# First weight of a fused attention and feed-forward kernel read in 8 pieces of 1024 columns, and two PE transposes a stage later

## The chip, the cores and the metric

The kernel runs on one core of one Trainium2 chip. A core has TensorE (PE, matrix products, with the loading of its stationary operand shown apart as PEld), VectorE (DVE), ScalarE (ACT), GpSimd (POOL) and SyncE (SP, which here only issues transfers). Each engine executes its own list of instructions in order and waits on semaphores where it needs another engine or a transfer. The metric is the device time of one execution in microseconds, the median of three runs.

## The reference

Block-sparse attention of 4 batches, 8 heads, 768 positions, 64 numbers per head, followed by layer norm and a feed-forward layer with a residual. In short:

```python
scores = q @ k.T / sqrt(64)                 # masked: blocks of 32 keys
mask = |block_i - block_j| <= 1, first and last block, 3 sampled blocks per query block
attn = exp(scores - max) / (sum + 1e-9)
x = attn @ v                                # 4 x 768 x 512
xn = (x - mean) / sqrt(var + 1e-6) * g_ln
out = x + relu(xn @ w_ch1) @ w_ch2          # w_ch1 512 x 2048, w_ch2 2048 x 512
```

The two weights come as 64-bit floats, the other tensors in 32 bits.

## The kernel before

**Steps and units.** A batch has 6 tiles of 128 queries. A unit is a pair of tiles, (1,2), (3,4) or (0,5); a step is one tile with one half of the heads, so unit 0 holds steps 0 to 3, unit 1 steps 4 to 7, and step 8 begins unit 2. A step multiplies scores (`scores` or, for the first and last block, `dense_scores`, into `ps`), takes maxima (L391), exponentials (L400), turns the weights (in the first eight steps on PE, L405; later by a DMA transpose), splits them into a high and a low half in 16 bits (`pt`, L410 and L417, or `pw`, L412 and L419) and multiplies with gathered V (`pa`, L454). Gathered V (`vg`) comes from DRAM by transfers of SP and by indirect transfers of POOL (L314); in steps 1 and 2 POOL first copies the maxima of the step to come (`fence`, L312), so that its gathers start no earlier. `rc` (L438) starts the normalisation of `pa` into x.

**Order.** The program's order is written out by hand in the loop over steps at the end of the kernel function: between the parts of a step stand positions pre, a, b, c, d, e, f, at which `hook` runs what is entered there. A weight piece is entered at one position; its load is issued by `pump` up to ten positions ahead (`LEAD`), as soon as its place is free.

**Weights.** A piece is one load of SP (L158) and one conversion: three integer operations on DVE (L172, L174, L176) make a 32-bit float `wf` of the 64-bit one, ACT writes its 16-bit high half (L186, into `w1h` or `w2h`), DVE its rest (L181, into `w1l` or `w2l`). `high()` and `low()` issue the last two when the loop calls them. Before, w1 has 16 pieces and w2 16, each 128 x 512 numbers or 512 KB. Pieces 0 to 2 are converted in step 0, pieces 3 to 31 at positions a, b, c, d of steps 1 to 7 and at a of step 8. Pieces are landed in `raw` (three buffers, shared with q, K and V of later batches) or in quarters of `w2h` and `w2l` that are still unused (`HOME`); `wf` has a pool of three.

**Feed-forward.** `layer_norm` is a generator of three stages: statistics; then the normalised input xn (L511) and, for units 0 and 1 (`XPE`), its four transposes on PE (L517, into `px`); then the copy of `px` into `xT` in two halves (L520, L521). Later units transpose by DMA. In step i the loop calls the stages of tile i-1: statistics behind b, the second at c, the third behind d. `ffn` makes up-projection (`pu`, L546, eight tiles of 24 matmuls), its relu in two halves (`hh` on ACT L558, `hl` on DVE L559) and down-projection (`pd`, L575), one matmul at a time, and the loop draws a planned number of them between its parts (`run`, `part`): for unit 0, 78 per step from step 4 on. `px`, `pu` and `pd` share three places in PSUM (`ps_f`), taken by turns; a tile must wait until the one three before it is read out. The V of batch 0 is staged in `st_hh` and `st_hl` (`hst`), whose memory becomes `hh` and `hl` when the feed-forward starts; stores to DRAM read it at the start of the program (L253).

Of the kernel before, what the change touches and what calls it, by code (L numbers as in the profile page):

```python
# [26 lines left out]
def sparse_attention_moe(  # L27
# [114 lines left out]

    def weight(i):
        if i < NW1:
            fq, c = divmod(i, CT)
            src = w1[c * P : (c + 1) * P, fq * 512 : (fq + 1) * 512]
            dh, dl = (w[:, c, fq * 512 : (fq + 1) * 512] for w in (w1h, w1l))
            return src, dh, dl, gs[:, c : c + 1]
        f = i - NW1
        return w2[f * P : (f + 1) * P, :], w2h[:, f, :], w2l[:, f, :], SW2  # L150

    HOME = {3: 3, 4: 4, 5: 5, 6: 6, 7: 7, 8: 0, 9: 1, 10: 2, 11: 3, 12: 4, 13: 5, 14: 6, 15: 7, 16: 1, 17: 2,
            18: 3, 19: 5, 20: 6, 21: 7, 22: 2, 23: 3, 24: 7, 25: 3, 26: 7, 27: 3}
# [14 lines left out]
    def convert_w(i):  # L168
        _, dh, dl, scale = weight(i)
        raw = wraw.pop(i).rearrange("p (e t) -> p e t", t=2)  # L170
        wf = wfp.tile([P, 512], I32, tag="wf", name=f"wf{i}")
        nc.vector.tensor_scalar(out=wf, in0=raw[:, :, 1], scalar1=3, scalar2=0x3FFFFFFF,  # L172
                                op0=ALU.logical_shift_left, op1=ALU.bitwise_and)
        nc.vector.scalar_tensor_tensor(out=wf, in0=raw[:, :, 1], scalar=-0x40000000, in1=wf,  # L174
                                       op0=ALU.bitwise_and, op1=ALU.bitwise_or)
        nc.vector.scalar_tensor_tensor(out=wf, in0=raw[:, :, 0], scalar=29, in1=wf,  # L176
                                       op0=ALU.logical_shift_right, op1=ALU.bitwise_or)
        f = wf.bitcast(F32)

        def to_low():  # L180
            nc.vector.scalar_tensor_tensor(out=dl, in0=f, scalar=scale, in1=dh, op0=ALU.mult,  # L181
                                           op1=ALU.subtract)
            wdone.append(i)

        def to_high():
            nc.scalar.activation(dh, f, AF.Copy, scale=scale)  # L186
# [18 lines left out]
    hst = [hp.tile([P, 4096], F16, tag=tag, name=f"st_{tag}") for tag in ("hh", "hl")]  # L205
# [291 lines left out]
    def layer_norm(u, k):  # L497
        b, t = u.b, u.ts[k]
        x = xs[b, t]
        nm = f"{b}_{t}"  # L500
        if k == 0:
            u.xT = lnp.tile([P, CT, 2, 2 * P], F16, tag="xT", name=f"xT{u.i}", bufs=2)
        bs = sm.tile([P, 6], F32, tag="bs", name=f"bs{nm}")
        mv = sm.tile([P, 4], F32, tag="mv", name=f"mv{nm}")
        nc.vector.bn_stats(bs, x)
        nc.vector.bn_aggr(mv[:, 0:2], bs)
        nc.scalar.activation(mv[:, 2:3], mv[:, 1:2], AF.Ln, bias=eps, scale=1.0)
        nc.scalar.activation(mv[:, 2:3], mv[:, 2:3], AF.Exp, scale=-0.5)
        yield
        xn = wfp.tile([P, DM], F32, tag="wf", name=f"xn{nm}")  # L510
        nc.vector.tensor_scalar(out=xn, in0=x, scalar1=mv[:, 0:1], scalar2=mv[:, 2:3],  # L511
                                op0=ALU.subtract, op1=ALU.mult)
        at = slice(k * P, (k + 1) * P)
        if u.i < XPE:
            pt = ps_f.tile([P, DM], F32, tag="pf", name=f"px{nm}")
            for c in range(CT):
                nc.tensor.transpose(pt[:, c * P : (c + 1) * P], xn[:, c * P : (c + 1) * P], ident)  # L517
# [5 lines left out]
        yield  # L523
# [9 lines left out]
    def ffn(u):  # L533
# [3 lines left out]
        for f in range(0, FT, 2):  # L537
            ph = ps_f.tile([P, 512], F32, tag="pf", name=f"pu{u.i}_{f}")
            for j in range(2):
                fs = slice((f + j) * P, (f + j + 1) * P)  # L540
                n = 0
                for c in range(CT):
                    for w, k in ((w1h, 0), (w1l, 0), (w1h, 1)):
                        while u.i == 0 and f // 4 * CT + c not in wready:
                            yield True
                        nc.tensor.matmul(ph[:, j * 2 * P : (j + 1) * 2 * P], w[:, c, fs],  # L546
                                         xT[:, c, k, :], start=n == 0 and j == 0,
                                         stop=n == 3 * CT - 1, skip_group_check=True)
                        n += 1
                        if n < 3 * CT or j == 0:  # L550
                            yield
            if late:
                late.pop()()

            def hidden(f=f, ph=ph):
                dh = hh[:, f : f + 2, :].rearrange("p f n -> p (f n)")
                dl = hl[:, f : f + 2, :].rearrange("p f n -> p (f n)")
                nc.scalar.activation(dh, ph, AF.Relu)  # L558
                nc.vector.scalar_tensor_tensor(out=dl, in0=ph, scalar=0.0, in1=dh,  # L559
                                               op0=ALU.max, op1=ALU.subtract)  # L560
# [69 lines left out]

    POS = ("pre", "a", "b", "c", "d", "e", "f")
    LEAD = 10
    PAT = {}

    def place(n):
        return n + (1 if n < NPE else LAG)
# [55 lines left out]
    def item(i, p, home, load, convert):  # L692
        n = index(i, p)

        def free():
            busy[home] -= 1

        def run_convert():
            gen = convert()
# [7 lines left out]

    def pump(now):
        blocked = set()
        for it in sorted(loads):  # L710
            n, _, home, load = it
            if n > now + LEAD:
                break
            if home in blocked or busy.get(home, 0) >= (3 if home == "raw" else 1):
                blocked.add(home)
                continue
            busy[home] = busy.get(home, 0) + 1
            load()
            loads.remove(it)

# [84 lines left out]
    i = 0  # L805
    while i < NS + LAG + FFLAG + 1 or ffq:
# [21 lines left out]
        if i < NPE:  # L828
# [5 lines left out]
            if i == 0:  # L834
# [181 lines left out]
```

## Time and profile before

| what | value |
|---|---|
| median of 3 runs | 801.84 us (798.68 to 802.06) |
| the profiled execution's own time | 802.09 us |
| its span | 800.1 us, 26387 instructions |
| PE busy | 684.5 us (86%), 11088 matmuls |
| DVE busy | 493.4 us (62%), 900 instructions |
| ACT busy | 465.4 us (58%), 1201 instructions |
| POOL busy | 173.8 us (22%) |
| HBM read and written | 89.18 MB and 12.95 MB |

Busy time is the sum over an engine's instructions; a share of the span is an average over stages with different limits. In the slices each digit is the busy share of a fortieth of the span in tenths. In the timeline a row has start, duration, engine, line, operation, what is written and read, and in brackets the idle time ahead of it with what ended it. The chain of waits is followed back from the last instruction, at each step to what released it or to the instruction ahead on its engine. "issue" means that the engine waited for nothing that the profile shows.

### The profile page before, as it was taken

To read this page: it belongs to the slowest core of one execution; us is meant where nothing else is said; L and a number is where in the kernel's file an instruction comes from. 1 tells how busy PE (TensorE), PEld (TensorE's weight loads), DVE (VectorE), ACT (ScalarE), POOL (GpSimd) and SP (SyncE) were. 2 spreads that over 40 slices of the span, in tenths; PEclk is the share of its full clock that TensorE was granted. 3 is DMA by queue.
4 is the path that set the end of the run, shared out by engine and by line. 5 is a ranking of instruction groups with operands and counts; after the bars stand their busy time and mean duration, and the time that the engine had idled before them with its cause. 6 is when DMAs were issued, how large, how long until landed. Compare 5 with 4: busy or idle time off the path is not lost.

```text
span 800.1 us, 26387 instructions
## 1 busy us (share of the span) xinstructions
PE 684.5 (86%) x11088; PEld 448.8 (56%) x11088; DVE 493.4 (62%) x900; ACT 465.4 (58%) x1201; POOL 173.8 (22%) x189
## 2 busy tenths in 40 slices
PE   0343376879887899999999899999999999999998
PEld 0232255536643584674865765847748658477573
DVE  5797979846756676556575765665666655444220
ACT  4764555345777786555767875566778655432110
POOL 0134410110205332203134231121343311110000
PEclk9999979799988999999999999999999999999999
DMA  8996646347969999997479999874699994541100
GB/s 287 267 298 204 181 126 201 114 113 150 226 146 207 221 231 205 212 188 185 112 169 216 234 201 245 174 191 115 129 212 212 199 193 103 141 101 29 53 1 27
DMA packets 196022, 136.36 MB, mean 170 GB/s; under 512 B 139584, under 2 KB 174912, under 8 KB 195904
## 3 DMA queue, kind: packets, MB, share of 16 engines
q1 hardware_dynamic: 186496, 110.69, 59.2%
q0 software_dynamic: 8448, 23.44, 12.3%
q8 instruction: 87, 1.43, 0.8%
q10 hardware_dynamic: 960, 0.54, 0.2%
q14 instruction: 31, 0.25, 0.1%
HBM read 89.18 MB, written 12.95 MB: 128 GB/s over the span
## 4 chain that ended last, share of the span: by engine, by line
PE 63%; DVE 17%; ACT 7%; DMA 6%; issue 5%; ACTq 1%; SPq 1%; DVEq 0%
PE pd L575 27%; PE pu L546 23%; PE pa L454 4%; PE ps L337 3%; DVE st L391 2%; DMA vdr<-vs 2%; PE pd L481 2%; DVE wf L174 2%; PE ps L343 2%; ACT ka L291 2%; PE ps L378 1%; DVE ka L235 1%; DVE wf L176 1%; DVE pw L419 1%; ACT ps L400 1%
## 5 line engine op out<-in xcount | busy, mean ns | idle before, releaser
L314 POOL DMA_INDIRECT vg<-vdr,vidx x176 | 172.4, 979 | 512.6 <-PE pa L454 334.4
L546 PE MATMUL pu<-xT,w1h 128*128 128x256 f16 x1536 | 264.5, 276 | 10.7 <-DMA xT<-xh 3.1
L546 PE MATMUL pu<-xT,w1l 128*128 128x256 f16 x768 | 211.8, 276 | 0.0
L546 PEld LDWEIGHTS <-w1h 128*128 128x128 f16 x1536 | 150.8, 99 | 29.0 <-issue 5.0
L575 PE MATMUL pd<-w2h,hh 128*128 128x512 f16 x384 | 148.6, 387 | 0.3 <-DVE hl L559 0.3
L575 PE MATMUL pd<-w2l,hh 128*128 128x512 f16 x384 | 148.1, 386 | 0.0
L575 PE MATMUL pd<-w2h,hl 128*128 128x512 f16 x384 | 147.8, 385 | 0.0
L400 ACT ACTIVATE ps<-ps,st 128x256 f32<-128x256 f32 (+1 forms) x176 | 85.6, 486 | 102.7 <-DVE st L392 78.4
L291 ACT COPY ka<-ka 128x128 f16 x576 | 123.2, 295 | 8.3 <-issue 6.8
L575 PEld LDWEIGHTS <-hh 128*128 128x128 f16 x768 | 71.7, 99 | 82.4 <-issue 8.7
L559 DVE SCALAR_TENSOR_TENSOR hl<-pu,hh 128x512 f16<-128x512 f32 x96 | 65.5, 687 | 71.2 <-ACT hh L558 62.3
L558 ACT ACTIVATE hh<-pu 128x512 f16<-128x512 f32 x96 | 56.1, 592 | 68.3 <-PE pu L546 65.0
L419 DVE TENSOR_TENSOR pw<-ps,pw 128x1024 f16<-128x1024 f32 (+1 forms) x56 | 64.3, 1148 | 46.2 <-ACT pw L412 37.4
L391 DVE TENSOR_REDUCE st<-ps 128x4 f32<-128x1024 f32 (+1 forms) x64 | 73.7, 1152 | 29.8 <-PE ps L378 17.3
L546 PEld LDWEIGHTS <-w1l 128*128 128x128 f16 x768 | 75.9, 99 | 16.6 <-issue 5.8
L454 PE MATMUL pa<-vg,pt 128*32 128x65 f16 (+1 forms) x4224 | 53.1, 200 | 13.8 <-issue 13.8
L575 PEld LDWEIGHTS <-hl 128*128 128x128 f16 x384 | 38.1, 99 | 47.0 <-issue 3.0
L454 PEld LDWEIGHTS <-pt 128*32 128x32 f16 x4224 | 44.7, 98 | 32.1 <-issue 30.2
L412 ACT CAST pw<-ps 128x1024 f16<-128x1024 f32 (+1 forms) x56 | 52.8, 944 | 0.5
L274 DVE TENSOR_TENSOR ql<-qr,qx 64x512 f16<-64x512 f32 x44 | 30.2, 686 | 26.3 <-ACT qx L273 19.3
L405 PE MATMUL ps<-ident,pw 128*128 128x128 f32 x64 | 13.1, 371 | 28.1 <-ACT pw L400 21.6
L581 DVE SCALAR_TENSOR_TENSOR ot<-pd,x 128x512 f32<-128x512 f32 x24 | 16.4, 686 | 32.1 <-PE pd L575 32.0
(83 smaller groups left out, 626.6 us busy)
## 6 DMA issues: line engine op xcount, KB each, us to landing
vg<-vdr SPq DMA_DIRECT2D x32, 390.0 KB
w2l<-w SPq DMA_DIRECT2D x13, 512.0 KB
va<-vdr SPq DMA_DIRECT2D x8, 780.0 KB
w2h<-w SPq DMA_DIRECT2D x12, 512.0 KB
out<-ot SPq DMA_DIRECT2D x24, 256.0 KB
qr<-qs SPq DMA_DIRECT2D x22, 256.0 KB
vg<-vdr SPq DMA_DIRECT2D x16, 292.5 KB
vdr<-vs SPq DMA_DIRECT2D x36, 130.0 KB
```

What stands on the lines that cost most here:

```text
L274: nc.vector.tensor_sub(ql[rows], raw[rows], qx[rows, j])
L291: nc.scalar.copy(kg[:, :, n], kxs[b, hg][:, :, bass.ds(val, 1)].rearrange("p j o q k -> p j (o q) k"))
L314: nc.gpsimd.indirect_dma_start(vg[:, qb - 4 * s.t, 1, :], None, src[:, :], bass.IndirectOffsetOnAxis(ap=vidx[:, qb : qb + 1], axis=0))
L391: nc.vector.tensor_reduce(out=s.st[:, 0 : s.m], in_=s.parts, axis=AX.X, op=ALU.max)
L400: nc.scalar.activation(to[:, k], s.parts[:, k], AF.Exp, bias=s.st[:, k : k + 1], scale=0.125)
L412: nc.scalar.copy(s.pw[:, 0, 0 : s.n], s.whole)
L419: nc.vector.tensor_sub(s.pw[:, 1, 0 : s.n], s.whole, s.pw[:, 0, 0 : s.n])
L454: nc.tensor.matmul(pa[gr * BLK : (gr + 1) * BLK, hl * 66 : hl * 66 + n], s.pt[:, ch + c, half, gr * BLK : (gr + 1) * BLK], s.vg[:, gr, c, ...
L546: nc.tensor.matmul(ph[:, j * 2 * P : (j + 1) * 2 * P], w[:, c, fs], xT[:, c, k, :], start=n == 0 and j == 0, stop=n == 3 * CT - 1, skip_gr ...
L558: nc.scalar.activation(dh, ph, AF.Relu)
L559: nc.vector.scalar_tensor_tensor(out=dl, in0=ph, scalar=0.0, in1=dh, op0=ALU.max, op1=ALU.subtract)
L575: nc.tensor.matmul(po, x[:, f, cols], w[:, f, :], start=f == 0 and n == 0, stop=f == FT - 1 and n == 2)
```

## The change

w1 now comes in 8 pieces of 1024 columns (1 MB each), so that w1 and w2 together have 24 pieces. Pieces 0 and 1 are converted in step 0, pieces 2 to 7 at positions a and c of steps 1 to 3, and the 16 pieces of w2, as wide as before, at a, b, c, d of steps 4 to 7; nothing is entered in step 8 any more. Pieces 0 and 1 are landed in rows of `w1l` and `w1h` that are written later, the others of w1 in two neighbouring quarters of `w2h` or `w2l`, so a place can be a tuple. The 32-bit float of a w1 piece stands in `st_hh` and `st_hl` by turns. And in `layer_norm` the second stage ends behind xn: the four transposes stand at the start of the third.

```diff
-    NW1, NW = CT * FT // 4, CT * FT // 4 + FT
+    hst = [hp.tile([P, 4096], F16, tag=tag, name=f"st_{tag}") for tag in ("hh", "hl")]
+    WC = 1024
+    NW1 = CT * DF // WC
+    NW = NW1 + FT
+    w1g, w1m = (x.rearrange("p c n -> p (c n)") for x in (w1h, w1l))
     def stage(i):
-        if i in HOME:
-            t, n = divmod(HOME[i], 4)
-            return (w2f, w2g)[t][:, n * 2048 : (n + 1) * 2048].bitcast(I32)
-        return rawp.tile([P, 1024], I32, tag="raw", name=f"wr{i}")
+        n = 2 * (WC if i < NW1 else DM)
+        if i < 2:
+            return (w1m, w1g)[i][:, DF : DF + 2 * n].bitcast(I32)
+        if HOME[i][0] == "raw":
+            return rawp.tile([P, n], I32, tag="raw", name=f"wr{i}")
+        t, k = divmod(HOME[i][0], 4)
+        return (w2f, w2g)[t][:, k * 2048 : k * 2048 + 2 * n].bitcast(I32)
...
+    HOME = {2: (4, 5), 3: (0, 1), 4: (2, 3), 5: (6, 7), 6: (4, 5), 7: (0, 1), 8: (2,), 9: (3,), 10: (6,), 11: (7,),
+            14: (2,), 15: (3,), 17: (7,), 19: (3,)}
+    HOME = {i: HOME.get(i, ("raw",)) for i in range(2, NW)}
...
     def convert_w(i):
-        wf = wfp.tile([P, 512], I32, tag="wf", name=f"wf{i}")
+        if i < NW1:
+            wf = hst[i % 2][:, 0 : 2 * WC].bitcast(I32)
+        else:
+            wf = wfp.tile([P, DM], I32, tag="wf", name=f"wf{i}")
...
         at = slice(k * P, (k + 1) * P)
+        yield
         if u.i < XPE:
             pt = ps_f.tile([P, DM], F32, tag="pf", name=f"px{nm}")
             for c in range(CT):
                 nc.tensor.transpose(pt[:, c * P : (c + 1) * P], xn[:, c * P : (c + 1) * P], ident)
-            yield
             src = pt.rearrange("p (c n) -> p c n", n=P)
...
-                        while u.i == 0 and f // 4 * CT + c not in wready:
+                        while u.i == 0 and f * P // WC * CT + c not in wready:
...
-    for i in range(3):
+    for i in range(2):
         load_w(i)
-    busy["raw"] = 3
+    busy.update({h: 1 for h in (0, 1, 2, 3, 6, 7)})
...
-    WPOS = [None] * 3 + [(i, p) for i in range(1, 9) for p in PAT.get(i, "abcd")]
+    WPOS = [None] * 2 + [(i, p) for i in range(1, 4) for p in "ac"] + [(i, p) for i in range(4, 8) for p in "abcd"]
```

`pump`, `item` and the step-0 code are changed to match (a tuple of places is free when each of its places is; piece 2 is no longer converted in step 0).

Three places in the engines' orders show what moves. On DVE, step 1 up to the second maximum (`st`), before; `wf` is the 32-bit float, `pt` the low half of step 1's weights:

```order
L172 TENSOR_SCALAR wf_630<-w2l 128x512
L174 SCALAR_TENSOR_TENSOR wf_630<-w2l,wf_630 128x512
L176 SCALAR_TENSOR_TENSOR wf_630<-w2l,wf_630 128x512
L181 SCALAR_TENSOR_TENSOR w1l<-wf_413,gs,w1h 128x512
L181 SCALAR_TENSOR_TENSOR w1l<-wf_485,gs,w1h 128x512
L417 TENSOR_TENSOR pt_636<-ps_371,pt_636 128x8x128
```

and with the change at the same place, where `st_hh` takes the part of `wf`:

```order
L183 TENSOR_SCALAR st_hh<-w2l 128x1024
L185 SCALAR_TENSOR_TENSOR st_hh<-w2l,st_hh 128x1024
L187 SCALAR_TENSOR_TENSOR st_hh<-w2l,st_hh 128x1024
L192 SCALAR_TENSOR_TENSOR w1l<-st_hh,gs,w1h 128x1024
L427 TENSOR_TENSOR pt_615<-ps_363,pt_615 128x8x128
```

The rest `w1l` of a piece now follows the integer operations of the same piece; before, those of two earlier pieces did. On PE, in step 6 around the transposes of tile 3 (`px_3`), before:

```order
L546 LDWEIGHTS w1l
L546 MATMUL pu_12_1985<-xT_869,w1l 128x256
L517 MATMUL px_3_2012<-ident,xn_3_2010 128x128 x4
L546 LDWEIGHTS w1h
L546 MATMUL pu_12_1985<-xT_869,w1h 128x256
```

and with the change:

```order
L555 LDWEIGHTS w1h
L555 MATMUL pu_14_1967<-xT_831,w1h 128x256
L528 MATMUL px_3_1987<-ident,xn_3_1953 128x128 x4
L555 LDWEIGHTS w1h
L555 MATMUL pu_14_1967<-xT_831,w1h 128x256
```

The transposes stand 19 matmuls of the up-projection later, in the middle of its last tile `pu_14` instead of in `pu_12`. Those of tile 4 in step 8 stand six matmuls of the down-projection later; else PE's order is the same. On DVE in step 8, from its maxima (`st`) to the normalisation (`rc`) of step 7's `pa`, before:

```order
L391 TENSOR_REDUCE st_2277<-ps_2260 128x1
L392 TENSOR_SCALAR st_2277<-st_2277 128x1
L181 SCALAR_TENSOR_TENSOR w2l<-wf_2241,w2h 128x512
L172 TENSOR_SCALAR wf_2318<-wr_2204 128x512
L174 SCALAR_TENSOR_TENSOR wf_2318<-wr_2204,wf_2318 128x512
L176 SCALAR_TENSOR_TENSOR wf_2318<-wr_2204,wf_2318 128x512
L181 SCALAR_TENSOR_TENSOR w2l<-wf_2318,w2h 128x512
L438 TENSOR_SCALAR rc_4_1_0_2435<-pa_2338 128x4
```

and with the change:

```order
L401 TENSOR_REDUCE st_2220<-ps_2203 128x1
L402 TENSOR_SCALAR st_2220<-st_2220 128x1
L192 SCALAR_TENSOR_TENSOR w2l<-wf_2184,w2h 128x512
L448 TENSOR_SCALAR rc_4_1_0_2372<-pa_2275 128x4
L449 RECIPROCAL rc_4_1_0_2372<-rc_4_1_0_2372 128x4
```

The conversion of one w2 piece is gone from there; it stands in step 7 now.

More of the change, by code (lines that the diff above doesn't have):

```diff
@@ L145, in weight @@
             fq, c = divmod(i, CT)
-            src = w1[c * P : (c + 1) * P, fq * 512 : (fq + 1) * 512]
-            dh, dl = (w[:, c, fq * 512 : (fq + 1) * 512] for w in (w1h, w1l))
-            return src, dh, dl, gs[:, c : c + 1]
+            at = slice(fq * WC, (fq + 1) * WC)
+            return w1[c * P : (c + 1) * P, at], w1h[:, c, at], w1l[:, c, at], gs[:, c : c + 1]
         f = i - NW1
         return w2[f * P : (f + 1) * P, :], w2h[:, f, :], w2l[:, f, :], SW2
-    HOME = {3: 3, 4: 4, 5: 5, 6: 6, 7: 7, 8: 0, 9: 1, 10: 2, 11: 3, 12: 4, 13: 5, 14: 6, 15: 7, 16: 1, 17: 2,
-            18: 3, 19: 5, 20: 6, 21: 7, 22: 2, 23: 3, 24: 7, 25: 3, 26: 7, 27: 3}
+    HOME = {2: (4, 5), 3: (0, 1), 4: (2, 3), 5: (6, 7), 6: (4, 5), 7: (0, 1), 8: (2,), 9: (3,), 10: (6,), 11: (7,),
+            14: (2,), 15: (3,), 17: (7,), 19: (3,)}
+    HOME = {i: HOME.get(i, ("raw",)) for i in range(2, NW)}
     wraw, whigh, wlow = {}, [], []
@@ L204, in sparse_attention_moe @@
     vsb = [const.tile([P, H, VR], F16, name="vs")]
-    hst = [hp.tile([P, 4096], F16, tag=tag, name=f"st_{tag}") for tag in ("hh", "hl")]
     vsf = [hst[i // 3][:, i % 3 * H * VR : (i % 3 + 1) * H * VR].rearrange("p (h d) -> p h d", d=VR)
@@ L522, in layer_norm @@
             return
-        yield
         xh = lnp.tile([P, DM], F16, tag="xh", name=f"xh{nm}", bufs=2)
@@ L632, in sparse_attention_moe @@
     LEAD = 10
-    PAT = {}
     def place(n):
@@ L695, in free @@
         def free():
-            busy[home] -= 1
+            for h in home:
+                busy[h] -= 1
         def run_convert():
@@ L709, in pump @@
         blocked = set()
-        for it in sorted(loads):
+        for it in sorted(loads, key=lambda it: it[:2]):
             n, _, home, load = it
@@ L713, in pump @@
                 break
-            if home in blocked or busy.get(home, 0) >= (3 if home == "raw" else 1):
-                blocked.add(home)
+            if any(h in blocked or busy.get(h, 0) >= (3 if h == "raw" else 1) for h in home):
+                blocked.update(home)
                 continue
-            busy[home] = busy.get(home, 0) + 1
+            for h in home:
+                busy[h] = busy.get(h, 0) + 1
             load()
@@ L748, in sparse_attention_moe @@
         work(convert_v(0, kt))
-    WPOS = [None] * 3 + [(i, p) for i in range(1, 9) for p in PAT.get(i, "abcd")]
-    WPOS = WPOS[:NW]
+    WPOS = [None] * 2 + [(i, p) for i in range(1, 4) for p in "ac"] + [(i, p) for i in range(4, 8) for p in "abcd"]
     assert len(WPOS) == NW
@@ L753, in sparse_attention_moe @@
         if at_w:
-            item(*at_w, HOME.get(i, "raw"), lambda i=i: load_w(i), lambda i=i: convert_w(i))
+            item(*at_w, HOME[i], lambda i=i: load_w(i), lambda i=i: convert_w(i))
     for b in range(1, B):
@@ L759, in sparse_attention_moe @@
             for c in range(2):
-                item(i + c, "b", "raw", lambda b=b, hg=hg, c=c: load_k(b, hg, c),
+                item(i + c, "b", ("raw",), lambda b=b, hg=hg, c=c: load_k(b, hg, c),
                      lambda b=b, hg=hg, c=c: convert_k(b, hg, c))
         for kt in range(NT):
-            item(v0 + kt, "d", "raw", lambda b=b, kt=kt: load_v(b, kt), lambda b=b, kt=kt: convert_v(b, kt))
+            item(v0 + kt, "d", ("raw",), lambda b=b, kt=kt: load_v(b, kt), lambda b=b, kt=kt: convert_v(b, kt))
     seen = set()
@@ L769, in sparse_attention_moe @@
                 if (s.b, t) not in ((0, first[0]), (0, first[1])):
-                    item(s.i - 2, "a" if s.i <= NPE else "b", "raw", lambda s=s, t=t: load_q(s.b, t), lambda s=s, t=t: convert_q(s.b, t))
+                    item(s.i - 2, "a" if s.i <= NPE else "b", ("raw",), lambda s=s, t=t: load_q(s.b, t), lambda s=s, t=t: convert_q(s.b, t))
     order = [s for s in steps if not (s.dense and s.j)]
@@ L846, in sparse_attention_moe @@
                 high()
-                convert_w(2)
                 keys(2)
@@ L851, in sparse_attention_moe @@
                 low()
-                busy["raw"] = 0
+                busy.update({h: 0 for h in (0, 1, 2, 3, 6, 7)})
             else:
```

## The prediction

> **What bounds the kernel now.** I read the page first: its span and its slices of 20 us.
>
> ```profile
> span 800.1 us, 26387 instructions
> ...
> PE   0343376879887899999999899999999999999998
> ...
> DVE  5797979846756676556575765665666655444220
> ```
>
> From the 14th slice on (about 260 us) PE is at 9 or 8 tenths, and nothing of the change lies there. All weights are converted in the first 168 us, where PE has 0 to 8 tenths and DVE up to 9. So the stretch to look at is steps 0 to 8. Its stages, by the view that cuts the span into windows (us busy of 20 for PE, PEld, DVE, ACT, POOL, then the granted clock, DMA share, GB/s):
>
> ```profile
> 20.00:40.00 20.00, 7.50 (x84) 4.11 (x81) 14.58 (x22) 15.86 (x43) 3.97 (x4) 1.00 0.91 267
> 80.00:100.00 20.00, 6.62 (x256) 4.90 (x244) 19.39 (x34) 11.84 (x28) 8.06 (x8) 0.93 0.65 181
> 120.00:140.00 20.00, 12.61 (x231) 10.58 (x229) 18.32 (x33) 11.75 (x22) 1.33 (x2) 0.95 0.65 201
> 140.00:160.00 20.00, 16.84 (x177) 10.47 (x178) 17.40 (x31) 7.66 (x14) 3.20 (x3) 0.79 0.35 114
> ```
>
> DVE is nearly full from 80 to 140 us (19.39 and 18.32 of 20), PE is not; around 150 us the two change places. The chain of waits, in order of time (start, us, what), shows where:
>
> ```profile
> 143.40 5.82 PE pu L546 x31
> 149.24 0.60 ACT hh L558
> ...
> 151.35 1.10 PE ps L405 x8
> ...
> 153.33 8.52 PE pd L575 x39
> ...
> 167.09 0.69 DVE w2l L181
> 167.79 0.08 DVE rc L438
> ...
> 173.34 5.68 PE pd L575 x21
> 179.02 0.90 PE ps L378 x16
> ```
>
> Ahead of 143.40 and of 173.34 stand the two transposes of the normalised input (`px`) in which PE waits. In the timeline, with the idle time ahead of each and what ended it:
>
> ```profile
> 142.31 1.09 PE L517 MATMUL px<-ident,xn 128*128 128x128 f32 x4 [9.70 <-DVE xn L511]
> ...
> 172.22 1.11 PE L517 MATMUL px<-ident,xn 128*128 128x128 f32 x4 [4.51 <-DVE xn L511]
> ```
>
> PE idles 9.70 and 4.51 us there, and the up-projection (`pu`) and down-projection (`pd`) matmuls behind are only queued behind `px`; they don't read it.
>
> **The change part by part.** The profiled execution took 802.09 us for its span of 800.1; the median of the runs is 801.84, 0.25 lower. I sum against 802.09.
>
> *A, wider pieces (steps 0 to 4).* One piece of 512 columns on DVE, up to the start of the next, and an operation of 1024 columns:
>
> ```profile
> 88.45 0.42 DVE L172 TENSOR_SCALAR wf<-w2l 128x512 int32<-128x512 int32 x1
> 88.91 0.69 DVE L174 SCALAR_TENSOR_TENSOR wf<-w2l,wf 128x512 int32<-128x512 int32 x1
> ...
> 90.24 0.74 DVE L181 SCALAR_TENSOR_TENSOR w1l<-wf,gs,w1h 128x512 f16<-128x512 f32 x1
> 90.90 0.42 DVE L172 TENSOR_SCALAR wf<-w2l 128x512 int32<-128x512 int32 x1
> ...
> 82.63 1.22 DVE L417 TENSOR_TENSOR pt<-ps,pt 128x1024 f16<-128x1024 f32 x1
> ```
>
> A piece is 90.90 - 88.45 = 2.45 us, of which L181 is 0.66 (90.24 to 90.90). 512 more columns cost a full-rate operation 1.22 - 0.69 = 0.53; L172 runs at about twice that rate, so 0.27. A piece of 1024 is an estimate from these: 2.45 + 0.27 + 3 x 0.53 = 4.31, against 4.90 for two. Eight save 8 x 0.59 = 4.7 us of DVE.
>
> [...]
>
> Most of it is not on the path, because of a wait that stands in step 2 anyway:
>
> ```profile
> 55.31 0.23 POOL L312 COPY fence<-st 1x4 f32<-1x4 f32 x1 [7.07 <-DVE st L392]
> ...
> 65.14 0.95 POOL L314 DMA_INDIRECT vg<-vdr,vidx  x1 [0.30 <-issue]
> ...
> 67.50 1.24 PE L454 MATMUL pa<-vg,pt 128*32 128x65 f16 x75 [1.15 <-issue]
> ...
> 68.77 0.16 DVE L438 TENSOR_SCALAR rc<-pa 128x4 f32<-128x4 f32 x1 [3.62 <-PE pa L454]
> ...
> 102.46 0.54 DVE L511 TENSOR_SCALAR xn<-x,mv 128x512 f32<-128x512 f32 x1
> ```
>
> POOL's gathers start when the maxima of step 2 (`st`, L392) are out and run back to back to 66 us; PE gets through `pa` only when they are done, and DVE waits 3.62 us for it. What DVE saves before that point is eaten there. The maxima themselves come later: a piece of 1024 without its L181 stands ahead of them (4.31 - 1.19 = 3.12) where one of 512 with its L181 stood (2.45), so +0.67 on the gathers and on `rc`. From there to xn of step 4 (102.46) both kernels convert nine halves; six of them are three pieces of 1024 now: -3 x 0.59 = -1.77. The last L181 falls behind xn: -0.6. And a new wait: at position a of step 3 the successor of L181 follows its own three integer operations directly, so DVE waits for ACT's conversion of 1024 columns in between, where two pieces used to cover each other. ACT's nearest rows:
>
> ```profile
> 79.64 0.72 ACT L186 ACTIVATE w1h<-wf,gs 128x512 f16<-128x512 f32 x1 [2.13 <-DVE wf L176]
> 80.27 0.99 ACT L410 CAST pt<-ps 128x1024 f16<-128x1024 f32 x1
> ```
>
> So between 0.99 (another operation of 1024) and 1.44 (twice L186); I take 1.2, nearer to the row of that width. In steps 1 and 2 that wait lies in DVE's waits for `pa` and beside the splitting of q. A = 0.67 - 1.77 - 0.6 + 1.2 = **-0.5**. Bounds: -2.3 if the gathers don't hold step 2 and the new wait is covered, +1.7 if that wait shows in a second step and is 1.44 long.
>
> Loads. The bytes are the same; the first two pieces put 2 MB ahead of the V stores where three put 1.5. The conversion of piece 0 now writes over V's staging, so it must wait for those stores:
>
> ```profile
> 18.96 2.79 SPq L253 DMA_DIRECT2D vdr<-st_hh  x6
> ...
> 25.27 0.42 DVE L172 TENSOR_SCALAR wf<-wr 128x512 int32<-128x512 int32 x1
> ...
> 132.83 0.69 DVE L176 SCALAR_TENSOR_TENSOR wf<-w2l,wf 128x512 int32<-128x512 int32 x1
> ```
>
> The stores are all issued by 21.75, 3.5 us ahead of piece 0; half a MB more takes 2.0 us at 267 GB/s. The tightest later load is that of 6c: its `raw` buffer is freed by the integer operations of 6a (133.5) and it is read at 139.2, behind the hl of 138.62 quoted below; half a MB at the 201 GB/s of that window is 2.6 us. I cost loads at 0; a late one shows with its rest, 1 to 3 us, on DVE.
>
> *B, first moved transpose (step 6).* 19 `pu` matmuls now stand ahead of `px`. The rows they hang on:
>
> ```profile
> 132.34 0.27 PE L546 MATMUL pu<-xT,w1l 128*128 128x256 f16 x1
> ...
> 138.62 0.69 DVE L559 SCALAR_TENSOR_TENSOR hl<-pu,hh 128x512 f16<-128x512 f32 x1 [1.08 <-ACT hh L558]
> ...
> 143.41 0.68 DVE L559 SCALAR_TENSOR_TENSOR hl<-pu,hh 128x512 f16<-128x512 f32 x1
> ```
>
> Seven end tile `pu_12` right behind 132.34. The next 12 start `pu_14`, which by turns of three in `ps_f` takes the place of `pu_8`, free after its hl at 139.3; they still run in PE's idle time. `px` then takes the place of `pu_10`, free at 143.41 + 0.68 = 144.1, that is 1.8 later than it started before. Then px 1.1 and the 12 matmuls that are left: the chain's 31 took 5.82, 0.188 each, so 2.25. End at 147.45 against 149.22: B = **-1.7**. Bounds: 0 if the later `px` holds xT and so DVE; -2.9 if those 12 run at the full clock, half of 0.188 each.
>
> *C, one piece fewer in step 8.* The last w2 half of before stands in 8a, ahead of `rc`, and its L181 ends when `rc` starts (167.09 + 0.69, above). `pa` was complete long before:
>
> ```profile
> 164.71 0.96 PE L454 MATMUL pa<-vg,pt 128*32 128x65 f16 x96
> ```
>
> Now 7d holds the last half, so `rc` follows `pa` at 165.7, and all behind it (statistics, xn, `px`) comes 2.05 earlier. C = **-2.05**; bound 0, if another wait stands there.
>
> *D, second moved transpose (step 8).* Six `pd` matmuls stand ahead of `px` now, in PE's wait. At full clock one is 0.218 (39 in 8.52): 1.3. The wait shrinks to 4.51 - 2.05 - 1.3 = 1.2. After 4.51 us idle the 21 behind took 5.68, 0.27 each: PE had slowed down. After a short gap it had not:
>
> ```profile
> 189.15 0.27 PE L546 MATMUL pu<-xT,w1h 128*128 128x256 f16 x1 [1.51 <-DVE ot L581]
> ...
> L546 PE MATMUL pu<-xT,w1h 128*128 128x256 f16 x1536 | 264.5, 276 | 10.7 <-DMA xT<-xh 3.1
> ```
>
> That is 0.27 us for a form that takes 276 ns on average (the page's group). So 15 x 0.218 = 3.3 remain of 5.68: D = **-2.4**; bound -1.3 if the clock falls all the same. [...]
>
> Sum: -0.5 - 1.7 - 2.05 - 2.4 = -6.65. Behind step 9 both kernels issue the same order on PE, DVE and ACT, chained through them and the K and V loads of the next batch; nothing there stands at a fixed time, so I carry it whole to the end. 802.09 - 6.65 = **795.4**.
>
> **The rivals.**
>
> 1. *Forecast*, all parts arrive: 795.4, between 792 and 798.
> 2. *The gain is lost again, or never made.* For: later stages with much DMA may give back a lead. Against: loads there are issued as buffers come free, which moves too. Half of it lost: 798.7. If an operation of 1024 costs two of 512, A is 1.77 worse and 797.2 is left; all lost, as when the later `px` holds DVE and the lead is given back: 801 to 802. Against the former stands the row of 1.22.
> 3. *Slower, through POOL and PE.* PE stalls in `pa` whenever gathers run beside it, as in step 2. Over the kernel that view of the waits has (total, times, longest):
>
> ```profile
> PE pa L454 <- issue: 13.8, 18, 2.9
> ```
>
> Steps shift by some us against each other; each further step in which `pa` falls on the gathers costs what step 2 has on DVE, 3.62. It decides from the second on: two even the gain out (802.7), three make it 806.3. Against: gathers wait for releases by `pa` itself, so they move along.
> 4. *Nothing from A, through the first conversion:* V stores late by more than their slack delay step 0, but step 2's wait of 3.62 takes that up: 796 to 798.
>
> **How the numbers follow.** Forecast 0.54, rival 2 0.30, rival 3 0.09, rival 4 0.07. 0.5% is 4 us, about what a measurement here can tell from no change: faster means below 797.8. The forecast is that nearly whole (0.52), rivals 2 and 4 by 0.10: faster 0.62. Slower means over 805.8: 0.07 of rival 3, 0.03 unnamed: 0.10. Same 0.28. Range: the lower bounds of the parts add to -2.3 - 2.9 - 2.05 - 2.4 = -9.65, 792.4, less 1.4 for the spread of runs: 791; above, the end of rival 2 and the first part of rival 3: 802.5.
>
> **What would show it.** A wide piece takes 4.2 to 4.4 us on DVE. `rc` of step 2 at 69 to 70, xn of step 4 near 102. `pu` matmuls between 139 and 142; `px` some 2 us behind xn; the last `pu` near 147. `rc` of step 8 right behind `pa`; PE's wait before the second `px` 1 to 2 us; the scores behind it (179.02 before) near 172.4. I am wrong in A if `rc` of step 2 moves earlier, in B if DVE waits for xT, and in carrying the sum on if a lead of 6 us at 180 us is not there at 300.

## The result, and the profile after

The kernel after takes 795.22 us (median of 6 runs, 792.73 to 796.43) against 801.95 us for the kernel before (median of 6, 798.68 to 807.32). The ratio is 0.9921, 95% interval 0.9895 to 0.9947: faster by 0.8%, 6.7 us. The profiled execution took 795.35 us against 802.09, 6.74 less.

The page of the kernel after, span and slices of 20 us:

```profile
span 793.2 us, 26337 instructions
...
PE   0333467897969799999999899999999999999997
...
DVE  4886979947856576656566765575666745444220
```

From the 15th slice on (about 280 us) PE is at 9 or 8 tenths up to the last slice; from the 9th to the 14th it goes between 9 and 6. What the change does directly is done by 180 us. The chain of waits (start, us, what):

```profile
144.36 1.12 PE px L528 x4
145.48 2.57 PE pu L555 x12
...
150.19 1.09 PE ps L415 x8
...
152.17 8.53 PE pd L584 x39
...
169.77 3.24 PE pd L584 x15
...
173.93 0.97 DVE st L401
```

Where 31 `pu` stood behind the first `px` there are 12, and 15 `pd` instead of 21 behind the second. The maxima behind them (`st`) start at 173.93, where they started at 179.94: 6.01 earlier. The rows of the timeline (start, us, engine, line, what; in brackets the idle time ahead and what ended it) at the places named in the prediction:

```profile
55.80 1.28 DVE L192 SCALAR_TENSOR_TENSOR w1l<-st_hl,gs,w1h 128x1024 f16<-128x1024 f32 x1
56.03 1.09 POOL L322 COPY fence<-st 1x4 f32<-1x4 f32 x1 [7.54 <-DVE st L402]
57.00 0.69 DVE L183 TENSOR_SCALAR st_hh<-w2h 128x1024 int32<-128x1024 int32 x1
...
60.12 1.41 DVE L284 TENSOR_TENSOR ql<-qr,qx 64x512 f16<-64x512 f32 x2
61.56 1.28 DVE L192 SCALAR_TENSOR_TENSOR w1l<-st_hh,gs,w1h 128x1024 f16<-128x1024 f32 x1
62.77 1.22 DVE L427 TENSOR_TENSOR pt<-ps,pt 128x1024 f16<-128x1024 f32 x1
...
66.47 0.95 POOL L324 DMA_INDIRECT vg<-vdr,vidx  x1 [0.30 <-issue]
...
68.71 1.03 PE L464 MATMUL pa<-vg,pt 128*32 128x65 f16 x59 [1.15 <-issue]
...
69.78 0.16 DVE L448 TENSOR_SCALAR rc<-pa 128x4 f32<-128x4 f32 x1 [5.80 <-PE pa L464]
...
82.67 1.29 DVE L192 SCALAR_TENSOR_TENSOR w1l<-st_hh,gs,w1h 128x1024 f16<-128x1024 f32 x1 [1.22 <-ACT w1h L197]
...
139.59 0.39 PE L555 MATMUL pu<-xT,w1h 128*128 128x256 f16 x1 [6.02 <-DVE hl L568]
...
144.36 1.12 PE L528 MATMUL px<-ident,xn 128*128 128x128 f32 x4 [2.04 <-DVE hl L568]
...
164.58 0.16 DVE L448 TENSOR_SCALAR rc<-pa 128x4 f32<-128x4 f32 x1 [1.15 <-PE pa L464]
...
169.11 0.66 PE L528 MATMUL px<-ident,xn 128*128 128x128 f32 x4 [1.27 <-DVE xn L521]
```

A wide piece takes DVE 60.12 - 57.00 for its integer operations and 62.77 - 61.56 for the last, 4.33 us. In step 2 the wait for `pa` grew from 3.62 to 5.80 us. At 3a DVE waits the new 1.22 us for ACT. Twelve `pu` run from 139.59 on in what was idle time, `px` waits 2.04 for its place, and in step 8 `rc` follows `pa`.

To compare kernels, I cut the first 180 us at six rows of DVE and one of PE and take the differences. The stages end at `rc` of step 1, `rc` of step 2, xn of step 4, xn of step 6, `rc` of step 7, `rc` of step 8, and the first score matmul behind the second `px` (the mark; its row in the timeline starts at 178.95 before and 172.94 after; the expectations take its start in the chain of waits, 179.02 and 173.01). Each row below is one trace. The record gives no number for the chip of the pair. All in us:

| kernel | chip | rc 1 | to rc 2 | to xn 4 | to xn 6 | to rc 7 | to rc 8 | to mark | mark |
|---|---|---|---|---|---|---|---|---|---|
| before | pair | 50.55 | 18.22 | 33.69 | 39.16 | 14.78 | 11.30 | 11.25 | 178.95 |
| after | pair | 50.60 | 19.18 | 32.58 | 39.48 | 13.39 | 9.35 | 8.36 | 172.94 |
| E1 transposes only | 11 | 50.41 | 17.99 | 33.55 | 39.31 | 13.40 | 11.30 | 8.35 | 174.31 |
| E2 pieces only | 11 | 50.19 | 19.19 | 32.56 | 38.98 | 14.70 | 9.33 | 9.65 | 174.60 |
| E3 step 6 back | 11 | 51.07 | 19.23 | 32.57 | 39.32 | 14.85 | 9.34 | 8.36 | 174.74 |
| E4 half back in 8a | 11 | 50.30 | 19.20 | 32.59 | 39.51 | 13.40 | 10.71 | 8.34 | 174.05 |
| before again (C1) | 9 | 49.85 | 14.54 | 33.70 | 39.80 | 13.39 | 11.32 | 12.22 | 174.82 |
| after again (C2) | 9 | 49.51 | 13.28 | 32.64 | 39.42 | 13.39 | 9.36 | 8.35 | 165.95 |
| split pieces (C3) | 9 | 49.77 | 14.50 | 33.57 | 38.85 | 13.40 | 9.35 | 8.35 | 167.79 |
| early gathers (C4) | 9 | 50.00 | 13.28 | 32.50 | 40.00 | 12.49 | 8.65 | 8.36 | 165.28 |
| both edits (E10) | 13 | 50.50 | 15.25 | 31.40 | 39.04 | 13.40 | 9.35 | 8.35 | 167.29 |

Between before and after the five stages behind `rc` of step 2 give -1.11, +0.32, -1.39, -1.95 and -2.89.

### The profile page after: what moved, and what is told of

Same layout as the page of the kernel before. It is cut to its first block, busy times and chain, and to the rows that moved or that the text cites. A ratio compares the mean times of both kernels' runs of the same rounds, so it can differ in the third digit from the quotient of the medians.

```text
span 793.2 us, 26337 instructions
## 1 busy us (share of the span) xinstructions
PE 682.7 (86%) x11088; PEld 448.8 (57%) x11088; DVE 489.4 (62%) x868; ACT 464.7 (59%) x1193; POOL 178.9 (23%) x189
## 4 chain that ended last, share of the span: by engine, by line
PE 63%; DVE 15%; ACT 9%; issue 6%; DMA 5%; SPq 2%; ACTq 1%; DVEq 0%
PE pu L555 25%; PE pd L584 25%; PE pa L464 5%; ACT ka L301 3%; PE ps L347 3%; DVE st L401 2%; PE pd L491 2%; ACT ps L410 2%; PE ps L388 2%; DVE pw L429 1%; PE ps L353 1%; DMA w2h<-ks 1%; DMA vdr<-vs 1%; ACT pw L422 1%; DVE ka L245 1%
## 5 line engine op out<-in xcount | busy, mean ns | idle before, releaser
L324 POOL DMA_INDIRECT vg<-vdr,vidx x176 | 176.0, 1000 | 501.5 <-PE pa L464 352.8
L555 PE MATMUL pu<-xT,w1h 128*128 128x256 f16 x1536 | 267.3, 277 | 15.9 <-DVE hl L568 6.4
```

What stands on the lines that cost most here:

```text
L324: nc.gpsimd.indirect_dma_start(vg[:, qb - 4 * s.t, 1, :], None, src[:, :], bass.IndirectOffsetOnAxis(ap=vidx[:, qb : qb + 1], axis=0))
```

## Experiments on the parts of the change

These four ran on one chip (number 11), with 30 runs of the kernel before there, median 802.36 us. Neither the kernel before nor the one after was traced on that chip, so the stages below are compared with the pair's. By their times alone the four can't be told from the kernel after: all their intervals overlap its 0.9895 to 0.9947.

**E1, the transposes alone.** The kernel before, with one line moved:

```
-        if u.i < XPE:
+        yield
+        if u.i < XPE:
             pt = ps_f.tile([P, DM], F32, tag="pf", name=f"px{nm}")
             for c in range(CT):
                 nc.tensor.transpose(...)
-            yield
```

> Kernel before with one edit: the PE transposes of the normalised input a stage later; pieces of 512 as before, last w2 half still in 8a. Mark: start of the 16 score matmuls behind the second px (179.02 before, 173.01 after). Theory 1 (three separate parts: B and D from the transposes, C from the piece gone from step 8, next to nothing from DVE's shorter work): B as in the change (-1.4) and D from six pd matmuls moved into PE's wait, which is still 4.51 - 1.3 = 3.2 us long: 15 pd behind px take 3.3 if PE keeps its clock, 4.1 if not. Mark at 175.2 to 176.0, time -3 to -4 us. Theory 2 (the gain is DVE's 4.7 us of saved conversion, the transposes only follow): mark within 0.5 of 179.0, time unchanged. Theory 3 (the transposes carry all of it): mark near 173, time -6 or more.

Ratio 0.9949 (0.9920 to 0.9978), median 797.53. The mark is at 174.31, 4.64 earlier than before: 0.9 past the best end of theory 1 (175.2), which already had the 15 `pd` at full clock. Of these, 0.45 is `px` itself at full clock, and 0.36 was there at xn of step 6.

```profile
170.49 0.66 PE L518 MATMUL px<-ident,xn 128*128 128x128 f32 x4 [3.22 <-DVE xn L511]
```

PE waited 3.22 us, and the four transposes behind took 0.66, not 1.11: its clock was still up (granted 1.00 from 170 to 180 us, where before has a mean of 0.83). From `rc` of step 8 to the mark it is 8.35 us, as in the kernel after, where PE waits 1.27. A shorter wait gave nothing more.

**E2, the wide pieces alone.** The kernel after, with the same line put back.

> Kernel after with the transposes put back where they were: wide pieces alone. Theory 1: xn of step 6 as after (141.8), px directly behind it and PE idle over 9 us there; rc of step 8 two us earlier than before + 0.2, near 165.8; PE then waits 4.5 - 2 = 2.5 us for the second px, and the 21 pd behind it take 4.5 to 5.7: mark (179.02 before, 173.01 after) at 176.0 to 177.2, time -2 to -3 us. Theory 2 (DVE's saved work is the gain): mark at 174.3 or earlier, time -5. Theory 3: mark near 179, no gain.

Ratio 0.9940 (0.9913 to 0.9967), median 798.81. Mark at 174.60, 4.35 earlier than before.

```profile
169.48 0.66 PE L527 MATMUL px<-ident,xn 128*128 128x128 f32 x4 [2.56 <-DVE xn L521]
...
170.14 4.53 PE pd L585 x21
```

(The second line is from the chain of waits.) With C alone the wait is 2.56 us and the clock stays up (granted 1.00 from 160 to 180 us): the 21 `pd` take 4.53 instead of 5.68. So each half of the change brings PE through step 8 at full clock by itself. E1 and E2 gain 4.64 and 4.35 at the mark, both together 6.01: the clock is gained once. The mark is 1.4 ahead of theory 1's range (176.0 to 177.2), too: of this, 0.45 is `px` at full clock and 0.70 was there at xn of step 6. Theory 2 is near this mark (174.3), but not by its reason: its 4.7 us would have to show up to xn of step 6, where E2 stands 0.70 ahead of the kernel before, 0.36 of that from `rc` of step 1 already. Theories 2 and 3 both fall.

**E3, only the transposes of step 6 back.** In the kernel after `if u.i != 1 or k != 0:` goes ahead of the moved `yield`, and a `yield` for that case stands behind the transposes again.

> Kernel after with only the transposes of step 6 put back ahead of the 19 up-projection matmuls; those of step 8 stay moved. Theory 1 (B is worth 1.4 and carries through): the last pu matmul ends at 149.4 (148.05 after), everything behind is 1.4 later, mark at 174.4, time +1.4 us on the kernel after. Rival (step 8 waits for DVE and not for PE, so B is eaten before the mark): pu late by 1.4, but rc of step 8 within 0.3 of 164.58 and mark within 0.3 of 173.0.

The stage from xn of step 6 to `rc` of step 7 takes 14.85 instead of 13.39, and the mark is 1.80 later, of which 0.47 was there at `rc` of step 1. B is worth 1.4 in this trace and reaches the mark. The rival falls. In the time it doesn't show: ratio 0.9930 (0.9899 to 0.9960), median 795.99.

**E4, the last w2 half back in 8a.**

```
+    WPOS[-1] = (8, "a")
```

> Kernel after with the last w2 half at position a of step 8 again, as before. Theory 1 (C is one piece's 2.45 us on DVE ahead of rc, less the wait for pa): rc of step 8 near 166.6 (164.58 after), xn two us later, PE waits 3.3 us for the second px instead of 1.3, 15 pd behind it take 3.3 to 4.1: mark at 175.0 to 175.8, time +2 to +3 us on the kernel after. Rival (the half has room in step 8 and C came from work moved elsewhere): rc within 0.5 of 164.6, mark within 0.5 of 173.0.

```profile
162.52 0.42 DVE L183 TENSOR_SCALAR wf<-wr 128x512 int32<-128x512 int32 x1
...
165.09 0.69 DVE L192 SCALAR_TENSOR_TENSOR w2l<-wf,w2h 128x512 f16<-128x512 f32 x1 [0.70 <-ACT w2h L197]
165.71 0.15 DVE L448 TENSOR_SCALAR rc<-pa 128x4 f32<-128x4 f32 x1
```

`rc` waits for the half again. From `rc` of step 7 to `rc` of step 8 it is 10.71 against 9.35: +1.36, not +2. The half was taken from 7d, whose last subtraction now fits ahead of the maxima, in a wait of DVE for PE; in the kernel before, 7d was full and that 0.6 us came on top (11.30). The mark is +1.11, from a start 0.30 earlier, so at 174.05 it stands ahead of theory 1's 175.0 to 175.8; PE waits 2.61 us for the second `px` and not 3.3, and `px` takes 0.66. Ratio 0.9938 (0.9905 to 0.9970), median 797.93.

## Experiments on DVE's saving and on the wait in step 2

**E5, wide pieces, narrow operations.** Places, loads and order as after; each of the four operations of a piece is issued for columns 0 to 511 and for 512 to 1023:

```
+        for r in halves:
-        nc.vector.tensor_scalar(out=wf, in0=raw[:, :, 1], ...)
+            nc.vector.tensor_scalar(out=wf[:, r], in0=raw[:, r, 1], ...)
...
+            for r in halves:
+                nc.scalar.activation(dh[:, r], f[:, r], AF.Copy, scale=scale)
```

> Kernel after, each wide piece converted by eight operations of 512 columns instead of four of 1024 (four in a row on each half: 3 integer operations twice, then both ACT conversions, then both subtractions); places, loads and order as after. So DVE has its 4.7 us of work back, and only that. Theory 1 (DVE's saving is nearly all off the path: up to rc of step 2 the wait for pa eats it, then three pieces count 0.59 each, less what ACT's shorter first conversion gives at 3a): rc of step 2 within 0.3 of 69.8, xn of step 4 0.5 to 1.8 later than 102.36, mark (start of the 16 score matmuls of step 9, 173.01 after) 0 to 1.8 later, time 0 to +1.8 us on the kernel after. Theory 2 (the saving is the gain): mark 4 us or more later, time +4 to +5 us.

**E6, early gathers.** The fence on POOL's gathers of step 2 is tied to an earlier row:

```
                 tail()
+                if i == 1:
+                    gather_v(steps[2], SimpleNamespace(st=x_of(0, steps[0].t)[:, 0:4]))
...
-                if i == 1:
-                    gather_v(steps[2], steps[2])
```

> Kernel after; the fence that holds POOL's gathers of step 2 back until its maxima are out is tied to the attention output of the step before instead (x, written at 51.5), so the gathers of steps 2 and 3 run from 52 to 62 instead of 56 to 67.4, in a time in which PE waits for ACT. Theory 1 (PE gets through pa only when the gathers are done, whatever holds them): PE's pa of step 2 starts at 61.3 and is through by 63 to 64.5 instead of 69.7; rc of step 2 near 65 to 66 (the conversion's DVE work of that step ends at about 64), 4 to 5 us earlier; how much of it is left at the mark (173.01) tells what the steps in between have to wait for: 0 to 4.5 us, most likely 2 to 4. Rival (pa waits for something else, such as its instructions or PE's own order, and not for gathers): rc of step 2 within 0.5 of 69.8, time unchanged.

Both ran on another chip (number 0), and neither could be read as meant: ratio 0.9901 (0.9871 to 0.9931) and 0.9867 (0.9832 to 0.9902), but the kernel before takes 795.96 us there, and `rc` of step 2 stood at 64.46 in E5, where theory 1 said 69.8. PE did not stall in `pa` at all, although E5's gathers ran beside it. So the pair and both edits were put on one chip.

**C1 to C4: before, after, E5 and E6 again on one chip (number 9).**

> The kernel before, unchanged, for its trace on the same chip as the next three. Two runs on another chip than the pair's had no stall of PE in pa of step 2 while POOL's gathers ran beside it, and there the kernel before was 6 us faster too (795.96 against 802.36). Theory G (the stall belongs to the chip that the run falls on): rc of step 2 either near 68.8 with a wait of 3 us or more for pa, or near 65 with none, and the same in all of after, split pieces and this one; time near 802 in the first case, 796 in the second. Theory P (the stall hangs on when pa meets the gathers): it may stand in some of the four and not in others.

> The kernel after, unchanged, on the same chip. Theory G: rc of step 2 near 69.8 where the kernel before stalls, near 64 where it doesn't. The whole change without the stall: A is then not held by pa, and xn of step 4 comes earlier than in the kernel before by more than the 0.1 us of the pair: -1.8 (three pieces at 0.59) or more. Time 6 to 8 us under the kernel before in either case.

> Wide pieces converted by operations of 512 columns, again, now beside the kernel after. Theory 1 (DVE's saved 4.7 us nearly all off the path): mark (start of the score matmuls of step 9) 0 to 1.8 us later than in the kernel after where pa stalls in step 2; without the stall DVE itself bounds steps 2 to 5, and it is 1.5 to 4 later. Theory 2: 4 or more later in both.

> Gathers of step 2 tied to the attention output of the step before, again, now beside the kernel after. Where the kernel after stalls in pa of step 2: rc of step 2 4 to 5 us earlier and 2 to 5 us at the mark. Where it doesn't: POOL's gathers are on no path there, rc of step 2 and the mark within 0.5 us of the kernel after, time the same.

Medians: before 796.90 (20 runs; C1, the same kernel, 796.31), after 786.40, split 790.14, early gathers 787.47. Ratios: after 0.9893 (0.9851 to 0.9936), split 0.9920 (0.9891 to 0.9948), early gathers 0.9890 (0.9850 to 0.9930). The rows of step 2 in the kernel after on that chip:

```profile
60.07 0.73 PE L464 MATMUL pa<-vg,pt 128*32 128x65 f16 x69
61.00 0.39 PE L464 MATMUL pa<-vg,pt 128*32 128x65 f16 x27 [0.20 <-issue]
...
62.79 0.15 DVE L448 TENSOR_SCALAR rc<-pa 128x4 f32<-128x4 f32 x1
...
65.56 1.65 POOL L324 DMA_INDIRECT vg<-vdr,vidx  x1 [0.30 <-issue]
...
75.80 1.28 DVE L192 SCALAR_TENSOR_TENSOR w1l<-st_hh,gs,w1h 128x1024 f16<-128x1024 f32 x1 [1.22 <-ACT w1h L197]
```

The gathers run to 67 us, and `pa` is through at 61.4 all the same; `rc` follows DVE's own work with no wait. None of the four traces here has the stall, none of the two on chip 0, and all six of the pair and of chip 11 have it. This speaks for theory G and against theory P: `pa` starts 3.9 us behind the first gather in C2 and 4.0 us behind it in the kernel after, yet only the latter stalls. Each chip was used for one set of runs only, so it isn't shown whether the stall belongs to the chip itself or to something else that was the same throughout a set.

Without the stall DVE's own work bounds step 2, and the change is worth more: 8.87 at the mark, of which 2.66 stand at xn of step 4 (0.34 of them already at `rc` of step 1). Not all of the rest is the stall: the stage to `rc` of step 7, where B stands, gains nothing here, and the last one gains 3.87 where the pair's gained 2.89, since PE's clock in C1 stayed at half up to 172 us (its mean from 170 to 180 us is 0.88 there and 1.00 in C2). Both hang on the moment at which the clock rises (below, under B). Split pieces (C3) lose 1.22 of the second column and 0.93 of the third again: 2.15 of DVE's 4.7 us are on the path up to step 4, and the mark is 1.84 later than after, within the 1.5 to 4 that theory 1 gave here (the medians lie 3.7 apart, and the intervals of the ratios overlap). In C4 the stage up to `rc` of step 2 is as long as after, as expected; its mark is 0.67 earlier, a little more than the 0.5 allowed. Its first `px` behind step 6 ran at full clock (0.66 us, and 12.49 in place of 13.39), the stage behind is 0.71 shorter, and the stages ahead are 0.93 longer together.

**E9, early gathers once more** (number 10):

> Gathers of step 2 tied to the attention output of the step before, a third time, in the hope of a chip on which pa stalls (three of four sets so far: stall on one chip in all four traces, none on two others). If pa stalls here: theory 1 (gathers beside it hold PE) has PE through pa of step 2 by about 63 instead of 68.7 to 69.7, since the last of the eight gathers then starts at 61 to 62; the rival (something else of that chip holds it) has rc of step 2 at 69 to 70 as in the kernel after. If pa doesn't stall here, the run says nothing on that, and rc of step 2 is near 63.

No stall (`rc` of step 2 at 62.74). Ratio 0.9836 (0.9753 to 0.9918) from 2 runs of it and 3 of before, of which there is no trace there. The gathers ran beside `pa` (60.19 to 62.52 us) and `pa` took 1.20 us, so this set is one without the stall; what ends a stall it can't tell. The 3 runs of the kernel before have a median of 800.63 us, where theory G had 796 without a stall; they are few, and why is open.

**E10, early gathers, and no wait for ACT in steps 1 and 3** (number 13):

```
                 hook(i, "a")
-                high()
+                if i not in (1, 3):
+                    high()
...
                 split_low(s)
+                if i in (1, 3):
+                    low()
```

> Early gathers as before, and in steps 1 and 3 ACT splits the transposed weights of the softmax (pt) ahead of the wide piece's conversion, and DVE subtracts for pt ahead of the piece's last operation: so DVE no longer waits 1.22 us behind three integer operations for ACT. Theory 1 (that wait of A is on the path in steps 1 and 3): no wait over 0.3 us on DVE ahead of the last operation of the pieces in 1a and 3a; rc of step 3 a further 1.2 earlier against rc of step 2; xn of step 4 at 92.9 to 94.2 where pa doesn't stall (95.3 to 95.8 in the three kernels with wide pieces there); 1.1 to 2.4 us less at the mark; time 0.986 to 0.982 of the kernel before. Rival (PE's pa or ACT takes the place of that wait): wait gone, xn of step 4 within 0.4 of 95.4. If the run falls on a chip where pa stalls, rc of step 2 tells of the gathers, too: near 62 to 63 if the gathers hold PE, 68 to 70 if something else does.

This chip stalls (in short pieces, and the kernel before takes 803.12 us there), so the run answers both questions.

```profile
47.29 1.22 DVE L427 TENSOR_TENSOR pt<-ps,pt 128x1024 f16<-128x1024 f32 x1 [1.06 <-issue]
...
62.55 1.01 POOL L324 DMA_INDIRECT vg<-vdr,vidx  x1 [0.30 <-issue]
...
64.46 1.25 PE L464 MATMUL pa<-vg,pt 128*32 128x65 f16 x76 [1.21 <-issue]
...
65.75 0.16 DVE L448 TENSOR_SCALAR rc<-pa 128x4 f32<-128x4 f32 x1 [1.88 <-PE pa L464]
...
78.64 1.28 DVE L192 SCALAR_TENSOR_TENSOR w1l<-st_hh,gs,w1h 128x1024 f16<-128x1024 f32 x1
```

The last gather ahead of `rc` ends at 63.56 instead of 67.42, 3.86 earlier; PE comes out of its stall at 64.46 instead of 68.71, 4.25 earlier; `rc` at 65.75 instead of 69.78, 4.03 earlier. `pa` starts at 61.05 here and at 61.27 in the kernel after, so PE follows the end of the gathers and not its own start, though the two traces are from different chips. That is not quite the 62 to 63 expected, since two gathers still ran beside `pa`. The wait of 1.22 at 3a is gone, and the stage to xn of step 4 takes 31.40 against 32.58: -1.18, nearly all of that wait. In step 1 the same edit gains nothing: the wait moves ahead of `pt`, where DVE waits 1.06 us, and `rc` waits for `pa`, 0.80 us. The range given for xn of step 4 holds only for a chip without the stall (97.15 here). Median 793.68, ratio 0.9858 (0.9819 to 0.9898): below both kernels of the pair, though its interval touches that of the kernel after (0.9895 to 0.9947, on another chip).

## Why the prediction was right, step by step

**The total** came out as forecast (795.4 against 795.22). At the mark the parts are: 0.05 at `rc` of step 1, then +0.96, -1.11, +0.32, -1.39, -1.95, -2.89, together -6.01, where 6.65 was forecast. The other 0.7 of the 6.74 comes behind the mark, by the drift below. The mechanisms were right in the main; that the total agrees within 0.2 us is luck. A came out 0.7 worse than forecast, B 0.3 and C 0.1 smaller, D 0.5 larger, and the lead moves by 3 us on its way to the end. Runs of the kernel after alone spread over 3.7 us.

**A (-0.5)** was +0.2 at xn of step 6. The term behind `rc` of step 2 is right: -1.77 - 0.6 + 1.2 = -1.17 was forecast up to xn of step 4, and -1.11 measured, with a wide piece of 4.33 us (4.31 forecast; its first operation takes 0.69, where one of 512 columns takes 0.42, the 0.27 that was taken) and a wait of 1.22 for ACT (1.2). The term ahead of it was too small: `rc` came 1.01 later, not 0.67; the fence came 0.72 later, as worked out, but took 1.09 us instead of 0.23, and the gathers' last row is 1.33 later (66.47 against 65.14). The long fence runs beside DVE's last operation on the wide piece (55.80, 1.28 us) and ends with it, at 57.1; in C3, where that operation is 512 wide, it takes 0.56. Whether the one holds the other up, and so costs step 2 part of the 1.01, these times don't show. The +0.32 between steps 4 and 6 has no term; over the eleven traces of the table that stage takes 38.85 to 40.00, and on chip 9 the change gives -0.38 there. What bounded A, that the gathers hold `pa`, holds on the pair's chip and on 11 and 13. On chip 9 the gathers don't hold step 2, and from `rc` of step 1 to xn of step 4 it is -2.32. That is the lower bound, -2.3, but by luck: of its two conditions only the first came true. The new wait at 3a is still 1.22 us in C2 (above), and in its place the two wide pieces of step 2, which the bound leaves out, save 1.26 (2 x 0.59 = 1.18). The upper bound, +1.7, is not what its condition gives: 0.67 - 1.77 - 0.6 + 2 x 1.44 is +1.2.

**B (-1.7)** had the right mechanism and the wrong size: -1.39 (E3: 1.46 for its undoing). The 12 `pu` took 2.57 us where 2.25 was taken, 0.214 each, because PE was slow the whole time (granted clock 0.50 from 140 to 148 us): the step that failed is the mean of 0.188 over a stretch in which the clock rose at the end (24 `pu` at 0.214, then 7 at 0.11). The lower bound halved the same mean: 12 `pu` at full clock are 1.3 us, which makes it -2.7 and not -2.9. On chip 9 B is worth nothing between C1 and C2: the stage takes 13.39 in C1, too, with the transposes where they were. There the clock rose earlier. PE's rows behind `px` in the kernel before, on the pair's chip, and then in C1:

```profile
142.31 1.09 PE L517 MATMUL px<-ident,xn 128*128 128x128 f32 x4 [9.70 <-DVE xn L511]
...
147.46 0.42 PE L546 MATMUL pu<-xT,w1l 128*128 128x256 f16 x1
...
148.49 0.27 PE L546 MATMUL pu<-xT,w1l 128*128 128x256 f16 x1
```

```profile
138.58 1.09 PE L517 MATMUL px<-ident,xn 128*128 128x128 f32 x4 [9.73 <-DVE xn L511]
...
141.16 0.42 PE L546 MATMUL pu<-xT,w1l 128*128 128x256 f16 x1
...
141.74 0.27 PE L546 MATMUL pu<-xT,w1l 128*128 128x256 f16 x1
```

A `pu` takes 0.42 us at half clock and 0.27 at full (the granted clock is 0.50 from 146 to 148 us before, and 1.00 from 142 to 144 us in C1). In C4, on C1's chip, with the transposes moved, the 12 `pu` all ran at full clock and the stage takes 12.49. So what B is worth varies from trace to trace with the moment at which the clock rises, and that moment was not in the forecast.

**C (-2.05)** was -1.95: 11.30 to 11.32 in every kernel of the table that has the half in 8a as before, 9.33 to 9.36 in those without it, E4 and C4 aside.

**D (-2.4)** was -2.89. The `pd` came as worked out (3.24 for 15; 3.3 forecast); the term left out is `px` itself, which took 0.66 at a granted clock of 1.00 (168 to 170 us after) instead of 1.11 at 0.53 (172 to 174 us before). That the clock stays up, on which the -2.4 rested, is shown for step 8 from both sides: waits of 1.27, 2.56 (E2), 2.61 (E4) and 3.22 (E1) left it up, 4.51 (before) and 4.52 (C1) did not. At what length between 3.22 and 4.51 us a wait begins to cost the clock is not shown, nor what brings it up again: `pu` turned fast 3 us after the start of `px` in C1 and 6 us after it in the kernel before (the rows under B).

**Carrying it to the end** was roughly right. The lead by the stores' last operation (`ot`) is 6.0 us at 182, 9.3 at 264, 6.2 at 321, 9.0 at 434, 7.9 at 597 and 6.9 at 789. It is neither lost nor kept: it moves by 3 us. That both kernels go on alike behind step 9 was too simple a reason.

**Rival 3** has its mechanism, and not its price. By the view of PE's waits in the kernel after:

```profile
PE pa L464 <- issue: 18.4, 18, 2.8
```

That is 4.6 us more than the 13.8 before, in as many pieces, so shifted steps do stall longer; yet a whole step's price of 3.62 for each did not show, since the lead behind the mark never fell below 6.0. That `pa` stalls whenever gathers run beside it did not hold: in C2 they ran beside it up to its end at 61.4 us, and its only idle time was 0.20 us. Rival 2 did not come, as the lead at the end shows, nor did rival 4: `rc` of step 1 is within 0.05 us.

What stays open: which rows make the lead move between 6 and 9 us behind step 9, the +0.32 between steps 4 and 6, what sets the moment at which the clock rises, and why PE stalls on some chips and not on others. On a chip that stalls the split pieces were not tried, so what DVE's saving is worth there rests on the sum of A alone.

## What to carry to other kernels

Before an engine's saved time is counted, look for a wait that it runs into on its way; here one wait of 5.8 us on one chip hides most of what is worth 2.3 us on another, so a gain should be read on more than one chip. Matmuls moved into a wait of PE gained their own time here (six `pd`, 1.3 us), and also the time that those behind them lost at half clock (1.6 us: `px` took 1.11 for 0.66, the 21 `pd` 5.68 for 4.53), once the wait was 3.2 us or less instead of 4.5; E1 and E2 each gained that second part, and both edits together gained it once. When an operation is made wider, look at the engine that converts its result: ACT took 0.72 us for 512 columns and 1.15 for 1024, DVE waited 1.22 us for the latter, and putting one independent operation in between took that wait away whole in step 3.

## What the runs showed of the chip

PE's stall in `pa` while POOL issues indirect gathers goes with the set of runs. On chips 11, 13 and the pair's `pa` gets through in pieces about every 0.7 or 1.4 us, and in all seven traces PE comes out 0.9 to 1.4 us behind the end of the last gather; on chips 0, 9 and 10 it does not stall. Whether that is the chip itself is not shown, as each had one set. The kernel before takes 802 to 803 us on the former and 796 to 797 on chips 0 and 9; the three runs on chip 10 (800.63) don't fit this. No engine, queue or semaphore that the profile shows ends these waits. A stall of 2.6 to 3.0 us in `pa` between 186 and 204 us stands in all 14 traces, with no gather beside it, and is something else.
